# A new order for the projection phase of a linear-attention and SwiGLU block, and other queues for its first weights

## The chip, the cores and the metric

The kernel runs on one core of a Trainium2 chip. The metric is the device time of one execution in microseconds (us); of a kernel's runs the median is taken. Less is better.

## The reference

Two branches read the same 2048 rows of 512 bf16 values, and their sum with the rows themselves is the output.

```python
def _A_ref(x, wqkv, wo):                      # x is layernormed
    H = 32; Dh = D // H
    q, k, v = ...                             # (x @ wqkv), 32 heads of 16
    phi = lambda t: jnp.where(t > 0, t + 1, jnp.exp(t)) + 1e-6
    pq, pk = phi(q), phi(k)
    kv = jnp.einsum("bhsd,bhse->bhde", pk, v)
    z = jnp.einsum("bhsd->bhd", pk)
    num = jnp.einsum("bhqd,bhde->bhqe", pq, kv)
    den = jnp.einsum("bhqd,bhd->bhq", pq, z)[..., None] + 1e-6
    return (num / den).transpose(...).reshape(B, S, D) @ wo

def _B_ref(x, w_gate, w_up, w_down):          # F = 1792
    return (jax.nn.silu(x @ w_gate) * (x @ w_up)) @ w_down

xn = _layernorm(x)
return x + _A_ref(xn, ...) + _B_ref(xn, ...)
```

## The kernel before

The 2048 rows are 16 tiles of 128 (t = 0 to 15). The program is a list of operations, each for one engine, with the keys that it reads and writes; `_Program` turns the keys into semaphore waits, and every engine runs its operations in the order of the list. So the order in the list is the order on each of the five engines and in its DMA queue. An operation stands still until what it reads is there, and all that is behind it on its engine stands still with it.

There are two phases. Phase 1 normalises the tiles, projects them to Q and K, applies phi and accumulates G = xn^T phi(K) over all tiles in four banks of PSUM (banks 0 to 3). Phase 2 walks through 56 pairs (gate and up, eight matmuls each; four chunks of 512 rows by 14 chunks of F), turns G into the attention's matrix on the way, and adds both branches per output tile.

Phase 1 is one text of words, run from left to right by `run`. A word is a letter and a tile number, with chunks of the contraction behind a colon where not all four are meant. The letters that matter here:

- SyncE's DMA queue: `l` loads a tile of x. `D` transposes a normalised tile by DMA (L396) into xnT. `T` loads a large weight: T0 and T4 the halves of w_gate, T1 and T5 those of w_up (896 KB each), T2 the V part of wqkv, T3 wo (512 KB each), T6 w_down (1792 KB).
- VectorE: `S` is a tile's statistics (bn_stats L251 and bn_aggr L254). `L` normalises a tile (L315). `C` subtracts the mean. `u` and `s` make phi(Q) and phi(K) (L457) out of the projection's bank and the clamped exp. `g`, `f` and `w` copy transposed rows out of PSUM, `a` writes the negated mean as a row (L365 with VectorE).
- ScalarE: `R` makes the inverse deviation (L258, L260), `r` further powers of it (L265, L267, L269), `y` and `x` are the exps of Q and K (L436 for tiles 0 to 2, L439 for the others), `e`, `h` and `Y` copy transposed rows out of PSUM (L388, L353), `M` a negated mean (L272).
- GpSimd: `n` and `m` clamp the exps of Q and K (L446), `P` normalises a tile (L330 and L333), `J` makes the scaled rows that G needs for tiles 0 to 2, `O` is `a` on GpSimd.
- TensorE: `c` turns a tile of x by a matmul with the identity (L371), `d` adds the negated mean to that (L379), `W` and `X` transpose (L345), `K` and `Q` are the projections (L418, one matmul for each of four chunks of the contraction), `G` is the accumulation (L467, four matmuls), `F` is a filler of 256 columns (L241), `U` is one of phase 2's pairs done ahead (L521).

Tiles 0 to 2 ("centred") are projected before they are scaled by the inverse deviation: the exp takes the deviation as its scale and bias. Tiles 0 and 2 are transposed on TensorE as raw x, tiles 1 and 3 there after centring or normalising, and tiles 4 to 15 by DMA. For phase 2 the tiles 0 to 2 are normalised later too and turned by D0, D1 and D2. U0 needs the columns of tiles 0 to 3.

A projection takes the next of the banks 4 to 7 in turn (K and Q of tile 2 use banks 0 and 1), so it waits until the `s` or `u` of the projection four places back has read that bank. G of a tile waits for its `s`. The first G waits for banks 0 to 3, which the tiles at the start have used.

The first loads are six each on SyncE's and ScalarE's queues: tiles 0 to 3 of x and the four chunks (128 rows of wqkv by 512 columns, 128 KB) of the Q and of the K weights. A word Q1 in that list is chunk 1 of Q's weights. Ahead of all of it on TensorE, seven fillers of 512 columns (L241) run while the first loads are under way.

Of the kernel before, what the change touches and what calls it, by code (L numbers as in the profile page):

```python
# [111 lines left out]
def bass_parallel_sum__linear_attn_block__swiglu_ffn__prompt_kernel(nc, A_x, A_wqkv, A_wo, B_x, B_w_gate, B_w_up, B_w_down, out):  # L112
# [5 lines left out]
    with contextlib.ExitStack() as es:  # L118
        E = es.enter_context

        def sb(name, shape, dtype):
            return E(nc.sbuf_tensor(name, shape, dtype))
# [3 lines left out]
        r2 = sb("r2", [P, NC], f32)  # L126
# [59 lines left out]
        def xload(eng, t):  # L186
            load(eng, ("x", t), x_sb[:, t, :], xin[t * P:(t + 1) * P, :])
# [22 lines left out]
        def wchunk(eng, i, c):  # L210
            load(eng, ("wqk", i, c), wqkv[:, c, i * D:(i + 1) * D], A_wqkv[c * P:(c + 1) * P, i * D:(i + 1) * D])

        for eng, text in (("sp", "x0 x2 Q1 x3 Q2 K1"),
                          ("act", "x1 Q0 Q3 K0 K3 K2")):
            for w in text.split():
                if w[0] == "x":
                    xload(eng, int(w[1:]))
                else:
                    wchunk(eng, int(w[0] == "K"), int(w[1:]))
# [331 lines left out]
        def run(text):  # L551
            words = [(w[0], int(w[1:].split(":")[0]), [int(c) for c in w.split(":")[1]] if ":" in w else None)
                     for w in text.split()]
            late = {t for k, t, _ in words if k == "z"}
            later.update({t: i for i, t in enumerate(t for k, t, _ in words if k == "u" and t in late)})
            for k, t, cs in words:
                steps[k](t) if cs is None else steps[k](t, cs)

        run("""
            S0 c0 l13 M1 R0 O0 l5 d0 S2 F1 l4 F1 l11 O2 S1 r0 e0 h0 R2 c2 d2 Q0:01 g2 Q0:3 Q2:1 h2 Q2:3 C1 J0 W1  # L560
            S3 r2 J2 R1 l14 K0:0 Q0:2 Q2:2 Q2:0 K2:3 r1 w1 K0:3 K2:1 K0:1 R3 L3 J1 T1 y0 K0:2 n0 y2 K2:02 l9 S13
            n2 l10 X3 x0 x2 S4 u0 K1:23 K1:01 R13 m0 s0 Y3 m2 P13 u2 x1 Q1:012 s2 Q1:3 R4 y1 Q3 m1 S9 K3:13
            K3:02 l7 l12 R9 y3 G2 s1 D13 L1 G0 P4 D4 L9 n1 n3 G1 K13 u1 x3 m3 Q13 u3 s3 S5 x13 D9 m13 S7 y13 R5
            s13 K4 l8 x4 G3 S10 P5 K9 m4 s4 x9 D5 n13 m9 Q4 G13 y4 G4 u13 R10 S14 K5 R14 n4 L10 R7 Q5 s9 L7 l15
            l6 x5 P14 Q9 D1 u4 y5 G9 S6 D10 D14 m5 K10 s5 R6 n5 P6 D7 L2 S11 Q10 u5 D6 y9 G5 D2 x10 y10 n9 m10
            T2 K14 u9 P0 s10 x14 K7 n10 S12 R11 u10 m14 x7 m7 T3 Q6 S8 y6 R12 G10 K6 s14 R8 P12 D12 n6 x6 Q7 s7
            S15 L8 R15 G7 m6 u6 y7 s6 Q14 y14 D8 G14 Q12 P11 K12 n7 u7 y12 Q8 L15 x12 n14 n12 D0 m12 u14 D11 K8
            u12 s12 y8 n8 G6 G12 x8 K11 u8 m8 D15 s8 Q11 x11 K15 T0 Q15 y11 G8 x15 m11 T5 s11 y15 n11 m15 G11 T4
            u11 T6 n15 s15 u15 U0 G15 U1
        """)  # L570

        def gt_evac(c, eng):
# [181 lines left out]
```

## Time and profile before

| | us |
|---|---|
| median of 3 runs | 212.77 (212.51 to 212.78) |
| profiled execution, its own time | 212.57 |
| span of its instructions | 211.3 |
| TensorE busy | 207.0 |
| VectorE busy | 124.5 |
| ScalarE busy | 68.4 |
| GpSimd busy | 67.2 |

PE is TensorE's matmul side, PEld its weight loads, DVE is VectorE, ACT ScalarE, POOL GpSimd and SP SyncE; SPq and ACTq are the DMA issues of these queues. Lines are numbered as in the kernel above. In a timeline a row has the start and the length in us, the engine, line and operation, what it writes and reads, the shape, the count, and in brackets the idle time before it with what ended it. A matmul's length contains its way through the array, so the next one starts earlier than the row before it ends; spacing is read from start to start. In a row of waits stand who waited for whom, the total in us, how often, and the longest. In a row of DMA issues the last number is the median time from issue to landing.

Phase 1 ends on TensorE with U0 (from 47.77 us), G15 and U1 (from 50.35 us).

### The profile page before, as it was taken

The numbers are of one execution on the slowest core, as the hardware profiler recorded it, in microseconds if no ns is written. First come the engines' busy times: TensorE is split into PE (matmuls) and PEld (weight loads), VectorE is DVE, ScalarE is ACT, GpSimd is POOL, SyncE is SP. The second block draws the span as 40 slices with busy tenths as digits, with TensorE's granted clock in tenths as the row PEclk, the third lists the DMA queues.
The fourth block names the chain that finished last, engine by engine and source line by source line (L and its number), as shares of the span: only waits on it lengthen the run. The fifth ranks groups of instructions, "written<-read, shape, count | busy, mean of one in ns | idle before, by whom it ended". The sixth has DMA issues, their size and how long they took to land.

```text
span 211.3 us, 2728 instructions
## 1 busy us (share of the span) xinstructions
PE 207.0 (98%) x994; PEld 97.0 (46%) x1013; DVE 124.5 (59%) x223; ACT 68.4 (32%) x146; POOL 67.2 (32%) x95
## 2 busy tenths in 40 slices
PE   7999999999999999999999999999999999999996
PEld 3534444444544444444444444444444444444455
DVE  3799998653996368454644673464457463625122
ACT  5994656554344333031221322130123031220000
POOL 3795688649950162202102021202202210000000
DMA  5963557599501201110101110111001111011101
GB/s 157 364 200 78 124 102 225 101 343 365 161 0 25 53 0 25 25 50 28 25 25 36 38 29 25 25 46 28 28 25 26 25 50 50 3 50 26 49 28 50
DMA packets 28733, 16.43 MB, mean 78 GB/s; under 512 B 18608, under 2 KB 28592, under 8 KB 28720
## 3 DMA queue, kind: packets, MB, share of 16 engines
q1 hardware_dynamic: 27856, 15.48, 26.2%
q10 hardware_dynamic: 864, 0.79, 1.1%
q8 instruction: 8, 0.13, 0.3%
q14 instruction: 5, 0.04, 0.1%
HBM read 9.96 MB, written 2.10 MB: 57 GB/s over the span
## 4 chain that ended last, share of the span: by engine, by line
PE 94%; ACT 3%; DMA 1%; issue 1%; DVE 1%; POOL 0%
PE pb L521 46%; PE pb L655 23%; PE pb L418 11%; PE pb L651 7%; PE pb L467 7%; ACT ef L436 1%; DMA x_sb<-in_A_x_dram 1%; PE pb L579 0%; PE pb L379 0%; PE pb L645 0%; DVE stats L251 0%; ACT rstd L260 0%; ACT lnv L258 0%; ACT xnT L353 0%; PE pb L241 0%
## 5 line engine op out<-in xcount | busy, mean ns | idle before, releaser
L529 ACT ACTIVATE sil<-pb 128x512 bf16<-128x512 f32 x56 | 33.4, 597 | 104.1 <-PE pb L521 102.5
L534 DVE TENSOR_TENSOR hT<-pb,sil 128x512 bf16<-128x512 f32 x56 | 38.2, 683 | 38.1 <-PE pb L521 37.5
L521 PE MATMUL pb<-xnT,wg 128*128 128x512 bf16 x224 | 57.8, 379 | 0.0
L521 PE MATMUL pb<-xnT,wu 128*128 128x512 bf16 x214 | 55.8, 379 | 0.5
L655 PE MATMUL pb<-wd,hT 128*128 128x512 bf16 (+2 forms) x247 | 51.1, 355 | 0.3
L612 POOL TENSOR_TENSOR pz<-pq,zbc 128x512 f32<-128x512 bf16 x16 | 22.2, 1392 | 91.4 <-DVE den L619 79.4
L655 PEld LDWEIGHTS pb<-wd,hT 128*128 128x128 bf16 x252 | 23.5, 98 | 25.0
L521 PEld LDWEIGHTS pb<-xnT,wu 128*128 128x128 bf16 x224 | 21.9, 98 | 25.9
L521 PEld LDWEIGHTS pb<-xnT,wg 128*128 128x128 bf16 x224 | 21.9, 98 | 25.8
L661 DVE TENSOR_TENSOR out_sb<-pb,x_sb 128x512 bf16<-128x512 f32 (+2 forms) x18 | 11.4, 632 | 35.7 <-PE pb L655 35.7
L418 PE MATMUL pb<-wqkv,xnT 128*128 128x512 bf16 x102 | 23.8, 379 | 0.5 <-ACT xnT L353 0.4
L439 ACT ACTIVATE ef<-pb 128x512 bf16<-128x512 f32 x26 | 15.3, 593 | 12.5 <-PE pb L418 12.5
L446 POOL TENSOR_SCALAR ef<-ef 128x512 bf16<-128x512 bf16 x26 | 16.0, 617 | 8.6 <-ACT ef L439 8.6
L651 PE MATMUL pb<-M,pk 128*128 128x512 bf16 (+2 forms) x72 | 16.8, 355 | 0.0
L418 PEld LDWEIGHTS pb<-wqkv,xnT 128*128 128x128 bf16 x104 | 10.1, 98 | 12.9 <-ACT xnT L353 0.9
L467 PE MATMUL pb<-pk,xn 128*128 128x512 bf16 x51 | 12.8, 379 | 0.1
L251 DVE BATCH_NORM_STATS2 stats<-x_sb 128x6 f32<-128x512 bf16 x16 | 10.8, 678 | 3.4 <-DMA x_sb<-in_A_x_dram 3.4
L634 DVE TENSOR_TENSOR pq<-pq,rden 128x512 bf16<-128x512 bf16 x16 | 12.6, 785 | 0.0
L619 DVE TENSOR_REDUCE den<-pz 128x32 f32<-128x512 f32 x16 | 10.8, 676 | 0.0
L490 POOL TENSOR_TENSOR zacc<-zacc,pk 128x512 f32<-128x512 f32 x8 | 10.2, 1278 | 0.6
L457 DVE SCALAR_TENSOR_TENSOR pk<-pb,ef 128x512 bf16<-128x512 f32 x13 | 8.8, 679 | 2.6 <-POOL ef L446 2.6
L457 DVE SCALAR_TENSOR_TENSOR pq<-pb,ef 128x512 bf16<-128x512 f32 x13 | 8.8, 683 | 2.5 <-POOL ef L446 2.4
(70 smaller groups left out, 112.6 us busy)
## 6 DMA issues: line engine op xcount, KB each, us to landing
x_sb<-in_A_x_dram SPq DMA_DIRECT2D x15, 128.0 KB, 4.7
out_dram<-out_sb SPq DMA_DIRECT2D x15, 128.0 KB, 1.7
wu<-in_B_w_up_dram SPq DMA_DIRECT2D x2, 896.0 KB, 6.8
wg<-in_B_w_gate_dram SPq DMA_DIRECT2D x2, 896.0 KB, 7.0
wd<-in_B_w_down_dram SPq DMA_DIRECT2D x1, 1792.0 KB, 14.6
wqkv<-in_A_wqkv_dram ACTq DMA_DIRECT2D x5, 128.0 KB, 4.7
wqkv<-in_A_wqkv_dram SPq DMA_DIRECT2D x1, 512.0 KB, 3.9
wo<-in_A_wo_dram SPq DMA_DIRECT2D x1, 512.0 KB, 4.8
```

The lines of the kernel that those rows point to most:

```text
L418: fns.append(lambda e, c=c, first=first, last=last: e.matmul(banks[b][:, :], src[:, c, t * P:(t + 1) * P], wqkv[:, c, col:col + D], start= ...
L439: K.add("act", lambda e: e.activation(buf, banks[b][:, :], ACT.Exp), r=[B(b)], w=[bkey])
L446: K.add("pool", lambda e: e.tensor_scalar(out=buf, in0=buf, scalar1=top, scalar2=0.0, op0=ALU.min, op1=ALU.max), r=[bkey] + tkeys, w=[bkey])
L457: K.add("dve", lambda e: e.scalar_tensor_tensor(out=dst, in0=val, scalar=low, in1=mid, op0=ALU.max, op1=ALU.add), r=keys + lkeys, w=[dkey])
L467: K.add("pe", [(lambda e, c=c: e.matmul(banks[c][:, :], src[:, t, c * P:(c + 1) * P], pk[:, t, :], start=first, stop=last)) for c in range ...
L521: fns.append(lambda e, c=c, b=b, w_=w_: e.matmul(banks[b][:, :], w_[:, c, fc * P:(fc + 1) * P], xnT[:, c, C * 512:(C + 1) * 512], start=(c ...
L529: K.add("act", lambda e: e.activation(sil[:, j % 2, :], banks[gb(j)][:, :], ACT.Silu), r=[B(gb(j))], w=[("sil", j % 2)])
L534: K.add("dve", lambda e: e.tensor_tensor(out=hT[:, C % 2, fc, :], in0=banks[gb(j) + 1][:, :], in1=sil[:, j % 2, :], op=ALU.mult), r=[B(gb( ...
L612: K.add("pool", lambda e: e.tensor_tensor(out=pz[:, t % 2, :].rearrange("q (g p) -> q g p", g=NG), in0=pq[:, t, :].rearrange("q (g p) -> q ...
L634: K.add("dve", lambda e: e.tensor_tensor(out=heads(pq[:, t, :]), in0=heads(pq[:, t, :]), in1=rden[:, i, :][:, :, None].broadcast_to([P, NH ...
L651: fns = [(lambda e, g=g: e.matmul(banks[bank][:, 0:hi - lo], pk[:, t, g * P:(g + 1) * P], M[:, g, lo:hi], start=(g == 0), stop=False)) for ...
L655: fns = [(lambda e, fc=fc: e.matmul(banks[bank][:, 0:hi - lo], hT[:, C % 2, fc, jj * P:(jj + 1) * P], wd[:, fc, lo:hi], start=False, stop= ...
```

## The change

Two lists of words are replaced by others; no function is changed. In the list of the first loads, Q2 goes from SyncE to ScalarE, K2 from ScalarE to SyncE, and K1, K0 and K3 change their places. The text of phase 1 has another order, and these words differ:

- one of two fillers `F1` is gone, the other stands ahead of `c0`;
- the negated mean of tile 2 is made by VectorE (`a2`) and not by GpSimd (`O2`);
- of the four copies of turned rows of tiles 0 and 2, the first half of tile 0 goes from ScalarE to VectorE (`e0` to `g0`), and of tile 2 the first half from VectorE to ScalarE (`g2` to `e2`) and the second from ScalarE to VectorE (`h2` to `f2`);
- tiles 1 and 10 are normalised by GpSimd (`P1`, `P10` for `L1`, `L10`), tile 0 by VectorE (`L0` for `P0`).

Q0 and Q2 with K0 and K2 are cut into chunks in another order; Q1, K1, Q3 and K3 are mostly whole. The order of the large weights was T1, T2, T3, T0, T5, T4, T6, with the transposes D12, D8, D0, D11 and D15 between T3 and T0. It becomes T1, T0, T3, T4, T2, T6, T5, all but T1 behind D11, with D0 between T4 and T2. U0 stood ahead of G15 and U1 behind it; now all G stand ahead of U0.

```diff
-        for eng, text in (("sp", "x0 x2 Q1 x3 Q2 K1"),
-                          ("act", "x1 Q0 Q3 K0 K3 K2")):
+        for eng, text in (("sp", "x0 x2 Q1 x3 K1 K2"),
+                          ("act", "x1 Q0 Q3 Q2 K0 K3")):
...
         run("""
-            S0 c0 l13 M1 R0 O0 l5 d0 S2 F1 l4 F1 l11 O2 S1 r0 e0 h0 R2 c2 d2 Q0:01 g2 Q0:3 Q2:1 h2 Q2:3 C1 J0 W1
-            S3 r2 J2 R1 l14 K0:0 Q0:2 Q2:2 Q2:0 K2:3 r1 w1 K0:3 K2:1 K0:1 R3 L3 J1 T1 y0 K0:2 n0 y2 K2:02 l9 S13
-            n2 l10 X3 x0 x2 S4 u0 K1:23 K1:01 R13 m0 s0 Y3 m2 P13 u2 x1 Q1:012 s2 Q1:3 R4 y1 Q3 m1 S9 K3:13
-            K3:02 l7 l12 R9 y3 G2 s1 D13 L1 G0 P4 D4 L9 n1 n3 G1 K13 u1 x3 m3 Q13 u3 s3 S5 x13 D9 m13 S7 y13 R5
-            s13 K4 l8 x4 G3 S10 P5 K9 m4 s4 x9 D5 n13 m9 Q4 G13 y4 G4 u13 R10 S14 K5 R14 n4 L10 R7 Q5 s9 L7 l15
-            l6 x5 P14 Q9 D1 u4 y5 G9 S6 D10 D14 m5 K10 s5 R6 n5 P6 D7 L2 S11 Q10 u5 D6 y9 G5 D2 x10 y10 n9 m10
-            T2 K14 u9 P0 s10 x14 K7 n10 S12 R11 u10 m14 x7 m7 T3 Q6 S8 y6 R12 G10 K6 s14 R8 P12 D12 n6 x6 Q7 s7
-            S15 L8 R15 G7 m6 u6 y7 s6 Q14 y14 D8 G14 Q12 P11 K12 n7 u7 y12 Q8 L15 x12 n14 n12 D0 m12 u14 D11 K8
-            u12 s12 y8 n8 G6 G12 x8 K11 u8 m8 D15 s8 Q11 x11 K15 T0 Q15 y11 G8 x15 m11 T5 s11 y15 n11 m15 G11 T4
-            u11 T6 n15 s15 u15 U0 G15 U1
+            F1 M1 c0 l13 S0 O0 S2 a2 R0 d0 r0 g0 c2 d2 R2 h0 e2 Q0:0 Q0:1 Q0:3 Q2:01 S1 Q0:2 r2 C1 R1 S3 r1 J0
+            W1 l4 K0:1 K2:01 l11 R3 J2 l9 f2 w1 Q2:3 Q2:2 l10 l14 K0:2 K0:0 K0:3 y0 L3 y2 l5 J1 K2:2 K2:3 X3 T1
+            n0 K1 n2 x0 S13 S4 x2 u0 m0 s0 l12 Y3 R13 m2 l8 u2 Q1 P13 K3 D13 x1 s2 Q3:2 S9 y1 R4 m1 Q3:013 s1 R9
+            G0 G2 x3 P4 S5 L9 y3 n1 G1 m3 u1 n3 D4 D9 K13 l6 P1 x13 R5 s3 u3 Q13 S14 R14 K4 G3 x4 y13 m13 Q4 s13
+            y4 S10 K9 S6 P5 m4 n13 l7 R10 R6 x9 n4 P10 G13 s4 G4 u13 S7 u4 D5 m9 s9 K5 D10 R7 S12 L7 P14 D14 Q5
+            x5 m5 y5 Q9 y9 s5 n5 G9 K10 G5 u5 n9 K14 S11 S8 x10 R12 P6 D7 m10 l15 u9 Q10 P12 Q7 s10 R8 x14 L8 D6
+            y7 L2 R11 m14 K7 y10 x7 D1 G10 s14 S15 n7 R15 n10 u7 K6 m7 u10 G14 Q14 x6 D8 L15 K8 s7 m6 y14 s6 P11
+            x8 n14 Q8 D12 G7 y8 K12 D2 m8 x12 D15 L0 u14 Q12 D11 s8 n8 y12 u8 Q11 y11 T0 n12 K15 u12 T3 G6 x15
+            m12 s12 T4 D0 n11 G8 Q6 y6 K11 T2 x11 m15 u11 Q15 n6 s15 m11 G15 y15 n15 G12 u6 s11 u15 G11 U0 T6
+            U1 T5
         """)
```

## The prediction

> **What bounds the kernel now.** I read the page first: how busy each engine is, and the chain of work that ended last.
>
> ```profile
> span 211.3 us, 2728 instructions
> PE 207.0 (98%) x994; PEld 97.0 (46%) x1013; DVE 124.5 (59%) x223; ACT 68.4 (32%) x146; POOL 67.2 (32%) x95
> ...
> PE 94%; ACT 3%; DMA 1%; issue 1%; DVE 1%; POOL 0%
> ```
>
> TensorE is busy for 207.0 of 211.3 us and is 94% of the chain. The change adds no matmul, so it can gain only where PE stands still, waits at a slow clock, or does filler. The waits of PE name all the places:
>
> ```profile
> PE pb L241 <- PEq L739: 0.8, 1, 0.8
> PE pb L418 <- ACT xnT L353: 0.4, 1, 0.4
> PE pb L379 <- POOL nmb L365: 0.2, 1, 0.2
> ```
>
> The first is the start of the program. The other two lie in the first 13 us, which the timeline of PE shows (start, length, line, count):
>
> ```profile
> 3.78 0.63 PE L371 MATMUL pb<-ident,x_sb 128*128 128x128 bf16 x4
> 4.64 0.61 PE L379 MATMUL pb<-ident,nmb 128*128 128x256 bf16 x2 [0.23 <-POOL nmb L365]
> 5.04 0.63 PE L241 MATMUL pb<-const-bfloat16-1.0 128*128 128x256 bf16 x2
> ...
> 5.89 0.46 PE L379 MATMUL pb<-ident,nmb 128*128 128x256 bf16 x2
> 6.19 1.24 PE L418 MATMUL pb<-wqkv,hT 128*128 128x512 bf16 x5
> ...
> 10.09 1.89 PE L418 MATMUL pb<-wqkv,hT 128*128 128x512 bf16 x7
> 12.36 1.90 PE L418 MATMUL pb<-wqkv,xnT 128*128 128x512 bf16 x8 [0.37 <-ACT xnT L353]
> 14.10 2.75 PE L467 MATMUL pb<-pk,hT 128*128 128x512 bf16 x12
> ...
> 47.77 1.03 PE L521 MATMUL pb<-xnT,wg 128*128 128x512 bf16 x4
> ...
> 50.35 1.03 PE L521 MATMUL pb<-xnT,wg 128*128 128x512 bf16 x4
> ```
>
> From 47.77 to 50.35 twelve matmuls start (U0's eight, G15's four), 0.215 us each, so a group of four (one K, Q or G word) costs 0.863 us with the few hundredths between instructions. From 12.36 on the groups follow without a hole. The row at 10.09 holds eight matmuls (K1 and Q1, one record missing), so PE had issued everything by 10.09 + 8 x 0.216 = 11.82 and lost 0.54 us until 12.36; the view says 0.37 because it counts from a matmul's modelled end. That wait was for tile 3's transposed rows (Y3 on ScalarE). The second loss is the filler: two F1 at 5.04, the next useful matmul at 5.47, so 0.43 us.
>
> **The filler.** One F1 goes; the other moves ahead of c0. There it costs about half of 0.43, 0.21 us, and c0 starts at 3.99 instead of 3.78. d0 waits for the mean row from GpSimd until 4.64 in any case, and that idle 0.23 us hides the moved F1 (without that cover it would cost 0.21). d0 stays at 4.64, c2 starts at 5.04 instead of 5.47: **gain 0.43**, if d2's mean row is there. It is now made by VectorE (a2) behind the second aggregate:
>
> ```profile
> 4.91 0.18 DVE L254 BATCH_NORM_AGGREGATE mv<-stats 128x2 f32<-128x6 f32 x1
> 6.29 0.42 DVE L390 CAST hT<-pb 128x256 bf16<-128x256 f32 x1 [0.40 <-PE pb L379]
> ```
>
> The trace has no such operation on VectorE. Its nearest row is this aggregate, also one column, 0.18 us; from below it could be half of that, from above twice. So a2 ends at 5.2 to 5.5, I take 5.3, and d2 wants it at 5.47. g0, the 0.42 us cast, follows it and ends near 5.7, before Q0:0 wants it at 5.87.
>
> **The slow clock.** d0's two matmuls take 0.40 us (4.64 to 5.04); d2's two, of the same shape, 0.30 (5.89 to 6.19), and the first projections behind them 0.216 each. PE's clock doubles at about 6.1 us. What moves ahead of that moment is done at the slow rate: d2 costs 0.40 and starts at 5.47, Q0:0 starts at 5.87 and takes 0.32 instead of 0.22. **Loss 0.21.** The remaining order needs the same matmuls and transposes, so PE has issued Q1's last at 11.60 instead of 11.82.
>
> **The weight chunks.** The order now uses the chunks as it dealt them:
>
> ```profile
> 1.25 2.39 ACTq L184 DMA_DIRECT2D wqkv<-in_A_wqkv_dram  x5
> 2.67 0.91 SPq L184 DMA_DIRECT2D wqkv<-in_A_wqkv_dram  x2
> ...
> wqkv<-in_A_wqkv_dram SPq DMA_DIRECT2D x3, 128.0 KB, 4.7
> ```
>
> Every chunk has 128 KB, so I let a slot keep its landing: issue plus 4.7 us. Q2 goes from SyncE's fifth slot (2.67, lands 7.4) to ScalarE's fourth (2.2, lands 6.9) and is wanted at 7.05; K1 takes the fifth slot, lands at 7.4 and is wanted at 7.5; K0 lands at about 7.6, wanted 7.7. Margins are 0.1 to 0.2 us; a chunk 0.3 late costs at most 0.2. I take nothing.
>
> **The wait at 12.36.** It ends with ScalarE's evacuation of tile 3:
>
> ```profile
> 5.32 0.63 ACT L388 ACTIVATE hT<-pb 128x256 bf16<-128x256 f32 x2
> 5.85 0.29 ACT L258 ACTIVATE lnv<-mv,eps 128x1 f32<-128x1 f32 x1
> 6.39 0.38 ACT L388 ACTIVATE hT<-pb 128x256 bf16<-128x256 f32 x1
> ...
> 8.63 2.77 ACT L436 ACTIVATE ef<-pb,lstd,rstd 128x512 bf16<-128x512 f32 x4
> 11.28 0.30 ACT L258 ACTIVATE lnv<-mv,eps 128x1 f32<-128x1 f32 x1
> ...
> 11.72 0.58 ACT L353 ACTIVATE xnT<-pb 128x512 bf16<-128x512 bf16 x1
> ```
>
> Before: e0 and h0 (0.53 for two), R2 (0.54), h2. After: R2 at 5.32, at the 0.44 that R13 takes (11.28 to 11.72), then h0 and e2 at 0.27 each: r2 can start at 6.30, where before h2's 0.27 ended at 6.66. ScalarE is 0.36 ahead and its next steps are the same, so the four exps start at 8.27 and end at 10.92 (0.66 each), and Y3 now stands before R13: 10.92 + 0.58 = 11.50, plus the 0.06 from 12.30 to PE's start at 12.36. PE's first use, K3, comes at 11.60. **The whole 0.54 goes**, with 0.04 to spare.
>
> K3 and Q3 then end at 13.33. G0 needs the banks that u2 and s2 free. Exps, minima and sums of tiles 0 and 2 keep their order, so s2 should end 0.36 sooner than before. VectorE before:
>
> ```profile
> 8.76 0.41 DVE L315 TENSOR_SCALAR xn<-x_sb,mv,rstd 128x512 bf16<-128x512 bf16 x1 [0.63 <-ACT rstd L260]
> ...
> 12.87 0.74 DVE L457 SCALAR_TENSOR_TENSOR pk<-pb,flo,ef 128x512 bf16<-128x512 f32 x1
> 13.53 0.68 DVE L251 BATCH_NORM_STATS2 stats<-x_sb 128x6 f32<-128x512 bf16 x1
> ...
> 14.35 0.72 DVE L457 SCALAR_TENSOR_TENSOR pk<-pb,flo,ef 128x512 bf16<-128x512 f32 x1
> 14.98 1.35 DVE L315 TENSOR_SCALAR xn<-x_sb,mv,rstd 128x512 bf16<-128x512 bf16 x2
> ```
>
> That makes 12.87 + 0.74 - 0.36 = 13.25. Next late after Y3, then, is s2, less than 0.1 us ahead of PE.
>
> **Sum of the head:** 0.43 - 0.21 + 0.54 = 0.76 us; the first G starts at 13.33 instead of 14.10.
>
> **The middle, to 48 us.** Both orders hold the same groups, so any loss must be a new wait. The tightest I find is Q13, whose bank Q1 leaves only when u1 has been summed. VectorE after: s2 at 12.51, S9 13.17, s1 13.99, S5 14.65, L9 15.47 (0.66 a sum, 0.82 a pair of statistics, from start to start as in those rows). L9 costs 0.41 as at 8.76 or half of 1.35 as at 14.98; u1's 0.74 ends at 16.6 or 16.88, and PE arrives at 13.33 + 4 x 0.863 = 16.78: no wait, or 0.1. The Trainium skill, page "SBUF — State Buffer", section "Who interferes with whom", says that VectorE in its two-port modes and GpSimd exclude each other for a whole instruction: by that rule the slow row holds, since GpSimd has m3 to do there, and 0.1 would be lost. I take 0.07, near the slow row, which stands at the same place of the old order. One normalisation less on VectorE (L1 and L10 go to GpSimd as P1 and P10, P0 comes back as L0) helps the same stretch; on GpSimd P1 stands ahead of m13, but s13 is wanted only by K9, four groups or 3.4 us after K13's end. P10 stands ahead of m9, whose sum s9 is wanted by G9, four groups behind K9. The last sum, s11, has Q15, G15 and G12 between K11 and G11, 2.6 us, against the 0.66 of an exp and the 0.74 of a sum with a minimum between them. I found no other place with less than 0.2 us (K4 behind s3).
>
> **Forecast.** 0.76 - 0.07 = 0.7 us. The profiled execution took 212.57 (span 211.3 and 1.27 around it), so 211.87; the median of the runs, 212.77, stands 0.20 over it, so **212.05**. 0.2% is 0.43 us, about what a measurement of this kernel can tell from no change.
>
> **Rival 1: the vector chain takes it back.**
>
> ```profile
> 15.00:35.00 20.00, 19.89 (x92) 9.04 (x93) 19.27 (x40) 12.52 (x34) 14.44 (x27) 1.00 0.52 128
> ```
>
> In this row of 20 us (busy PE, weight loads, DVE, ACT, POOL) VectorE works for 19.27. If it can't come 0.7 sooner, small waits return 0.4 to 0.7 of the gain; with 0.5 the time is 212.55. Against it speaks that its load falls and its first part is 0.36 ahead; for it, that margins are tenths. 16%.
>
> **Rival 2, slower: D0 stuck behind weights.** Before, T0 is the last but three on SyncE and D0 had gone long before it. Now the order is D11, T0, T3, T4, D0, and U0 needs tile 0's columns.
>
> ```profile
> 34.41 6.45 SPq L396 DMA_TRANSPOSE xnT<-xn  x5
> 40.91 0.58 SPq L184 DMA_DIRECT2D wg<-in_B_w_gate_dram  x1
> ...
> 42.08 0.51 SPq L184 DMA_DIRECT2D wg<-in_B_w_gate_dram  x1
> ...
> wg<-in_B_w_gate_dram SPq DMA_DIRECT2D x1, 896.0 KB, 5.2
> ...
> wg<-in_B_w_gate_dram SPq DMA_DIRECT2D x1, 896.0 KB, 8.8
> ...
> wd<-in_B_w_down_dram SPq DMA_DIRECT2D x1, 1792.0 KB, 14.6
> ...
> 35.84 0.77 POOL L333 TENSOR_SCALAR xn<-x_sb,nm,rstd 128x512 bf16<-128x512 bf16 x1
> ```
>
> P11 stands behind m6, and K6 is the 23rd group behind 13.33 and ends at 33.2; with an exp, a minimum and the 0.77 of the last row, xn of tile 11 is there near 35.8, 0.8 sooner than before; a transpose takes SyncE 1.29 (6.45 for five), so T0 is issued at 37.1, lands 5.2 later at 42.3, T3 1.4 later (two loads of 896 KB landed 46.1 and 50.9 with one between: 2.4 each, so 1.4 for 512 KB), T4 at 46.1, D0 by 47.4. U0 comes at 13.33 + 40 x 0.863 = 47.9: hidden by 0.5. The Trainium skill, page "DMA: Bandwidth & Descriptors", section "Queues, rings and completion order", says that one queue's descriptors are consumed in ring order on each DMA engine, by which D0 can't overtake T4. If T0 goes out 1 us later and each load takes a third longer, as wd's 1792 KB did (57.2 - 50.9 = 6.3 by the last DMA row), D0 lands near 50, PE loses 2 us, and the time is 212.05 + 2 = 214.0, slower. It decides from a landing at 47.9, and turns the sign from 48.6. The load that is now last, T5, is no such case: the last before, wd, landed at about 42.6 + 14.6 = 57.2; T0 goes 3.8 sooner, T2 and T3 with 2.8 us of bytes come behind it, so T5 lands near 56 to 57, and its first user, the eighth pair of the second phase, comes 7 x 1.73 behind U0, at 60. 13%.
>
> **Rival 3: it doesn't do what it says.** Y3 or a chunk comes 0.3 late and half of the 0.54 stays: 212.05 + 0.27 = 212.3, still faster. 12%.
>
> **How the numbers follow.** Forecast 59%, the rivals 16, 13 and 12. Low end: 0.76 off the lowest run shown, 212.51, so 211.75. High end: rival 1 at its worst and the first 0.1 of a loss, 212.85. Faster 0.70: the forecast and rival 3. Same 0.15: rival 1. Slower 0.15: rival 2 and the worst of rival 1.
>
> **What would show it.** L241 once at 3.8, c2 near 5.04; Y3's evacuation near 10.9 and ahead of L258; no wait of PE for xnT before L467, which starts near 13.3; second-phase gate matmuls (L521) of U1 near 49.6. Wrong: a PE wait for DVE between 14 and 45, or one for the transposes (L396) ahead of L521 near 48.

## The result and the profile after

The changed kernel takes 211.96 us (median of 6 runs, 211.80 to 212.02) against 212.70 before (6 runs, 212.51 to 212.78). The ratio is 0.9966, with a 95% interval from 0.9953 to 0.9978: faster by 0.34%, against the 0.34% that 212.05 meant. A second series gave 211.94 against 212.56, a ratio of 0.9967 (0.9956 to 0.9978). So the medians differ by 0.74 us in the first series and by 0.62 in the second. The profiled execution took 212.02, 0.55 less than that of before.

The page of the changed kernel, three lines:

```profile
span 210.7 us, 2744 instructions
...
PE 207.8 (99%) x1012; PEld 96.6 (46%) x1012; DVE 124.4 (59%) x224; ACT 68.0 (32%) x145; POOL 67.8 (32%) x96
...
PE 97%; DMA 1%; DVE 1%; issue 0%
```

ScalarE and GpSimd have left the chain. The waits of PE, all that the view names:

```profile
PE pb L241 <- PEq L739: 0.8, 1, 0.8
PE pb L379 <- DVE nmb L365: 0.2, 1, 0.2
```

The wait for xnT is gone, and a short one for VectorE's mean row (a2) is new. The timeline of PE:

```profile
3.99 0.63 PE L371 MATMUL pb<-ident,x_sb 128*128 128x128 bf16 x4
...
4.83 0.39 PE L371 MATMUL pb<-ident,x_sb 128*128 128x128 bf16 x4
5.42 0.39 PE L379 MATMUL pb<-ident,nmb 128*128 128x256 bf16 x2 [0.20 <-DVE nmb L365]
5.75 1.73 PE L418 MATMUL pb<-wqkv,hT 128*128 128x512 bf16 x6
...
7.62 2.33 PE L418 MATMUL pb<-wqkv,hT 128*128 128x512 bf16 x10
...
11.73 1.89 PE L418 MATMUL pb<-wqkv,xnT 128*128 128x512 bf16 x8
13.46 0.81 PE L467 MATMUL pb<-pk,hT 128*128 128x512 bf16 x3
...
47.99 1.03 PE L521 MATMUL pb<-xnT,wg 128*128 128x512 bf16 x4
...
49.72 1.03 PE L521 MATMUL pb<-xnT,wg 128*128 128x512 bf16 x4
```

K3 starts at 11.73, where before the first matmul on tile 3 came at 12.36: 0.63 us. The first G is 0.63 ahead (13.46 for 14.10) and U1 is 0.63 ahead (49.72 for 50.35). PE's last matmuls, too, are 0.64 ahead (a row at 207.91 for one at 208.55). So in these two executions all of the gain is made by 11.73 us, and neither the middle nor the end changes it. ScalarE, then VectorE, in their timelines:

```profile
5.71 0.64 ACT L388 ACTIVATE hT<-pb 128x256 bf16<-128x256 f32 x2
...
8.24 2.79 ACT L436 ACTIVATE ef<-pb,lstd,rstd 128x512 bf16<-128x512 f32 x4
10.91 0.60 ACT L353 ACTIVATE xnT<-pb 128x512 bf16<-128x512 bf16 x1
11.39 0.31 ACT L258 ACTIVATE lnv<-mv,eps 128x1 f32<-128x1 f32 x1
```

```profile
5.21 0.16 DVE L365 TENSOR_SCALAR nmb<-mv 128x1 bf16<-128x1 f32 x1
...
12.50 0.74 DVE L457 SCALAR_TENSOR_TENSOR pk<-pb,flo,ef 128x512 bf16<-128x512 f32 x1
...
15.42 0.59 DVE L315 TENSOR_SCALAR xn<-x_sb,mv,rstd 128x512 bf16<-128x512 bf16 x1
15.94 0.74 DVE L457 SCALAR_TENSOR_TENSOR pq<-pb,flo,ef 128x512 bf16<-128x512 f32 x1
```

Y3 (L353) ends at 11.51, 0.22 ahead of K3. Its chain no longer decides; what does is told below.

### The profile page after: what moved, and what is told of

It reads as the page before. It is cut to its first block, busy times and chain, and to the rows that moved or that the text cites. A ratio compares the mean times of both kernels' runs of the same rounds, so it can differ in the third digit from the quotient of the medians.

```text
span 210.7 us, 2744 instructions
## 1 busy us (share of the span) xinstructions
PE 207.8 (99%) x1012; PEld 96.6 (46%) x1012; DVE 124.4 (59%) x224; ACT 68.0 (32%) x145; POOL 67.8 (32%) x96
## 4 chain that ended last, share of the span: by engine, by line
PE 97%; DMA 1%; DVE 1%; issue 0%
PE pb L521 46%; PE pb L655 23%; PE pb L418 13%; PE pb L651 7%; PE pb L467 7%; DMA x_sb<-in_A_x_dram 1%; DVE stats L251 1%; PE pb L579 0%; PE pb L645 0%; PE pb L345 0%; PE pb L379 0%; DVE mv L254 0%; DVE out_sb L661 0%; DVE nmb L365 0%
## 5 line engine op out<-in xcount | busy, mean ns | idle before, releaser
L521 PE MATMUL pb<-xnT,wu 128*128 128x512 bf16 x224 | 57.8, 379 | 0.0
L651 PEld LDWEIGHTS pb<-M,pk 128*128 128x128 bf16 x72 | 6.8, 98 | 7.4
```

The costliest lines, as they stand in the source:

```text
L521: fns.append(lambda e, c=c, b=b, w_=w_: e.matmul(banks[b][:, :], w_[:, c, fc * P:(fc + 1) * P], xnT[:, c, C * 512:(C + 1) * 512], start=(c ...
L651: fns = [(lambda e, g=g: e.matmul(banks[bank][:, 0:hi - lo], pk[:, t, g * P:(g + 1) * P], M[:, g, lo:hi], start=(g == 0), stop=False)) for ...
```

## The experiments

Each experiment has its own runs of the kernel before on the same chip; their medians lay between 212.56 and 212.62.

**One word of the old order.** Y3 ahead of R13, nothing else:

```diff
-K1:23 K1:01 R13 m0 s0 Y3 m2 P13
+K1:23 K1:01 Y3 R13 m0 s0 m2 P13
```

> The kernel before with one word moved: Y3 ahead of R13. Theory (the gain is the wait for tile 3's rows, ended by ScalarE): Y3 starts at 11.28 instead of 11.72, PE's first use comes at 11.92 instead of 12.36, so 0.44 us sooner; 212.7 becomes 212.26. Rival (the gain comes from the order of the middle, with one normalisation less on VectorE, and the wait at 12.36 is made up for later): within 0.1 of 212.7.

Measured 212.25, ratio 0.9982 (0.9973 to 0.9991). The timelines of ScalarE and of PE:

```profile
11.28 0.60 ACT L353 ACTIVATE xnT<-pb 128x512 bf16<-128x512 bf16 x1
```

```profile
11.94 1.90 PE L418 MATMUL pb<-wqkv,xnT 128*128 128x512 bf16 x8
13.68 1.67 PE L467 MATMUL pb<-pk,hT 128*128 128x512 bf16 x7
...
50.14 1.03 PE L521 MATMUL pb<-xnT,wg 128*128 128x512 bf16 x4
```

Y3 and PE's first use come when they were expected (11.28 and 11.92). Half of the change's gain, 0.37 of 0.74 us, is to be had by this one move, and the wait for tile 3 is shown to have cost time. In this execution not all of it is kept: the first G is 0.42 ahead of the kernel before, U1 only 0.21 (50.14 for 50.35), because two projections of the old middle now wait for their transposes (0.05 us at 26.68, 0.14 at 37.19).

**The fillers alone.**

```diff
-S0 c0 l13 M1 R0 O0 l5 d0 S2 F1 l4 F1 l11
+F1 S0 c0 l13 M1 R0 O0 l5 d0 S2 l4 l11
```

> The kernel before with the change's fillers alone: one F1 gone, the other ahead of c0. Theory: PE comes to the wait for tile 3's rows 0.2 to 0.4 us sooner and waits there that much longer, because ScalarE's chain is as before: 212.7, no change within 0.1. Rival (fillers are a term of their own, as the sum in the prediction has them, 0.43 less 0.21): 212.5 or less.

Measured 212.46, ratio 0.9993 (0.9984 to 1.0002): not to be told from no change. The number alone does not decide: 212.46 lies where the rival had it, but it is only 0.16 below the 212.62 of the kernel before beside it. The profiled execution is the slowest of the eleven (212.69), and its timeline of PE shows where the freed time went:

```profile
5.57 0.64 PE L379 MATMUL pb<-ident,nmb 128*128 128x256 bf16 x2
6.49 1.18 PE L418 MATMUL pb<-wqkv,hT 128*128 128x512 bf16 x4 [0.29 <-ACT rstd L260]
```

d2's two matmuls would be issued by 6.0, and the first projections start at 6.49: the missing fillers have become a wait there, earlier than the one expected at tile 3. The trace puts it down to rstd, which those projections do not read; they want chunk Q1, which landed at 6.36 in this execution (at 6.00 in the profile of before).

**Both together.**

> Both edits of the two kernels beside it. Theory: Y3 ends at 11.86 and PE comes to it earlier than that, so the first K3 or Q3 starts at 11.92 as with Y3 alone, and G2 stays behind s2 (end 13.61) at 13.66: 212.26, no better than Y3 alone by over 0.1. Rival (the terms add): 212.26 less 0.2 to 0.4, so about 212.0.

Measured 212.52, ratio 1.0001 (0.9983 to 1.0019; one run at 214.54 makes the interval wide). The terms do not add, but 212.26 is missed too. In its profile the first projections start at 6.58, behind a chunk that landed at 6.45. Whether the fillers' absence makes the old head worse or these executions had late landings stays open.

**The filler back in the new order.**

```diff
-S2 a2 R0 d0 r0 g0 c2 d2
+S2 a2 R0 d0 F1 r0 g0 c2 d2
```

> The changed kernel with the second F1 put back between d0 and c2. Theory (PE waits for a2 and for the chunks in any case): 0.1 to 0.2 us of filler fall into those waits, 211.96 within 0.1. Rival (the filler's time is a term of its own): 0.2 more, 212.2 or above.

Measured 212.11, ratio 0.9975 (0.9966 to 0.9984): 0.15 over the changed kernel's 211.96, between the two expectations and not to be told from either. PE in its profile:

```profile
5.05 0.42 PE L241 MATMUL pb<-const-bfloat16-1.0 128*128 128x256 bf16 x1
5.26 0.63 PE L371 MATMUL pb<-ident,x_sb 128*128 128x128 bf16 x4
5.69 0.63 PE L379 MATMUL pb<-ident,nmb 128*128 128x256 bf16 x2
6.11 1.57 PE L418 MATMUL pb<-wqkv,hT 128*128 128x512 bf16 x6
...
13.62 0.59 PE L467 MATMUL pb<-pk,hT 128*128 128x512 bf16 x2
```

Here c2's four matmuls still run slowly (0.63, where the changed kernel's take 0.39), the first projection starts 0.36 later (6.11 for 5.75), and the first G only 0.16 later (13.62 for 13.46), as much as K1's chunk landed later (7.73 for 7.57).

**The halves of the change.** The new order up to the first G, and the old one behind it:

```diff
 ... Q3:2 S9 y1 R4 m1 Q3:013 s1 R9
-G0 G2 x3 P4 S5 L9 y3 n1 G1 m3 u1 n3 D4 D9 K13 ...
+y3 G2 l7 L1 G0 P4 D4 L9 n1 n3 G1 K13 u1 x3 m3 ...
```

> The new order up to the first G with the new queues, and the old order from there on (L1, L10, P0 and the old places of the large weights and of U0). Theory (all of the gain is in the first 13.5 us): 212.0 to 212.15; up to 0.15 may go where K4 now takes the bank that s3 frees last. Rival (the middle and the end bring it): 212.5 or more.

Measured 212.94, ratio 1.0014 (1.0005 to 1.0022). It is not faster: the theory's number is too low by 0.8 to 0.9 us. The waits of PE:

```profile
PE pb L418 <- DMA wqkv<-in_A_wqkv_dram: 0.5, 1, 0.5
PE pb L418 <- DMA xnT<-xn: 0.4, 1, 0.4
```

In this execution a late chunk spoiled the head (K1 landed at 8.11, first G at 14.01), but the rest lost time as well: from the first G to U1 it took 36.96 us (14.01 to 50.97) where before took 36.26 (14.10 to 50.35). 0.17 of that is K4's wait for s3, and the rest K10's wait for its transpose D10 (the second row; from start to start it is 0.51). D10 landed 3.24 us after its issue, where in the kernel before it took 2.49. There two other transposes took as long (D14 3.34, D7 3.25), and PE did not wait for them; why one lands later than another was not followed.

The seam also makes something that is in neither order: l7, which the old order has ahead of D13 and the new one behind D9, stands between D13 and D4, and D4 lands at 18.34 (17.48 before, 17.35 in the changed kernel). So what this half loses is not shown to be the old order's doing alone. The other half, the old head with the new rest:

> The old order and queues up to the first G, and the new order from there on. Theory (the gain is in the head alone): 212.7 within 0.1. Rival (the middle brings part of it): 212.5 or less.

Measured 212.55, against 212.60 of the kernel before beside it, ratio 1.0002 (0.9994 to 1.0011): nothing, as the theory had it. From the first G (14.04) to U1 (50.30) it takes 36.26 us, exactly as before: both orders of the middle are dense when PE comes as late as before. So neither half is faster by itself. The new head wins the time; the old rest, as it is joined on here, hands it back, and the new rest keeps it.

**Which words keep it.** D1 behind D10 and D14, and in a second kernel also P1 for L1:

```diff
-x5 P14 Q9 D1 u4 y5 G9 S6 D10 D14 m5
+x5 P14 Q9 u4 y5 G9 S6 D10 D14 D1 m5
```

```diff
-G2 l7 L1 G0 P4 D4 L9 n1 n3 G1
+G2 l7 G0 P4 D4 L9 n1 n3 P1 G1
```

> The kernel with the new head and the old rest, with one word moved: D1 behind D10 and D14 instead of ahead of them in SyncE's queue. Theory (that kernel lost its gain at K10, which waited for D10 behind D1, a transpose that only phase 2 needs): D10 is issued 1.25 us sooner, the wait of 0.5 us or more goes, 212.94 becomes 212.2 to 212.45. Rival (the late chunk at 8.16 us of its profile was the loss): 212.9.

> The same with P1 behind n3 on GpSimd instead of L1 on VectorE. Theory (the other wait, 0.17 us of K4 for s3, comes from L1's 0.74 us on VectorE ahead of u1, u3 and s3): it goes too, 212.05 to 212.25. Rival (P1 puts GpSimd's minima late instead): no better than D1 alone.

Measured 212.84 (ratio 1.0013, 1.0002 to 1.0024) and 212.93 (1.0019, 1.0010 to 1.0027). Both theories fall. The first rival's 212.9 is met, but not for its reason: no chunk was late in this profile, the first G starts at 13.57. With D1 moved the wait at K10 is gone, but the chain finds the next places. PE loses 0.28 us at 18.16, where D4, the transpose behind l7, landed at 18.02 and s3 ended at 18.00, and 0.34 at three later ones, all of them transposes. So U1 starts at 50.43, 0.08 later than before, though the first G came 0.53 sooner. In the second kernel, with P1 ahead of m3, it is the rival's way: the first G is at 13.24, 0.86 sooner than before, and U1 at 50.53, 0.18 later. Its waits of PE, then VectorE's timeline:

```profile
PE pb L418 <- DVE pk L457: 0.5, 1, 0.5
```

```profile
17.47 0.69 DVE L457 SCALAR_TENSOR_TENSOR pk<-pb,ef 128x512 bf16<-128x512 f32 x1 [0.85 <-POOL ef L446]
```

VectorE idles 0.85 us ahead of s3 for a minimum that GpSimd does behind P1, and K4 waits 0.5 for that s3. The new order has P1 behind m3. Which set of its moves is needed to keep the gain is not settled; these two are not enough, and all three of these kernels have l7 at the seam.

**The queues.** The changed kernel with the old lists of first loads:

```diff
-("sp", "x0 x2 Q1 x3 K1 K2"), ("act", "x1 Q0 Q3 Q2 K0 K3")
+("sp", "x0 x2 Q1 x3 Q2 K1"), ("act", "x1 Q0 Q3 K0 K3 K2")
```

> The changed kernel with the chunks of Q and K on the old queues. Theory (PE takes each chunk within 0.1 us of its landing): Q2 lands at about 7.57 and K1 at 8.0 instead of 7.04 and 7.57, so K0:1 starts at about 8.07 instead of 7.62 and nothing behind it has that much to spare: 0.45 us more than the changed kernel, 212.4. Rival (the clock and the order of the engines set the head, the deal is cover only): 212.0.

Measured 212.44, ratio 0.9999 (0.9990 to 1.0008): the 212.4 that was expected. But its profile does not show the expected wait. The chunks landed up to 0.9 us early in it (K1 at 7.27), and PE's clock turned late:

```profile
5.12 0.63 PE L371 MATMUL pb<-ident,x_sb 128*128 128x128 bf16 x4
5.55 0.63 PE L379 MATMUL pb<-ident,nmb 128*128 128x256 bf16 x2
5.98 1.89 PE L418 MATMUL pb<-wqkv,hT 128*128 128x512 bf16 x6
7.71 0.39 PE L345 MATMUL pb<-ident,hT 128*128 128x128 bf16 x4
...
13.77 0.59 PE L467 MATMUL pb<-pk,hT 128*128 128x512 bf16 x2
```

From 4.72 on PE has no hole here, c2 and d2 run at the slow rate, and so do the first two of the six projections from 5.98 (0.43 us each, 0.22 behind them). The first G starts at 13.77, 0.31 later than in the changed kernel, with no wait to put it down to: in this execution the slow clock held the head. So the kernel ran again, beside the changed one.

> The changed kernel with the old queues once more, because the chunks of its first profile landed up to 0.9 us sooner than in all the others. Theory: with landings as usual (fifth slot 7.4 to 8.1) its K0:1 waits for K1 until about 8.1 and the first G starts at 13.9, 0.4 later than the changed kernel beside it; the median is 0.3 to 0.5 above it. Rival (the deal does nothing): the same as the changed kernel within 0.1.

> The changed kernel once more, beside the three others on one chip. Both theories: 211.96 within 0.15. Theory (the head is held by landings and not by the clock): the first G starts at 13.3 to 13.7 whenever PE's clock turns. Rival (the slow clock is a term, as the prediction had it): a turn 1.5 us later than the 4.6 us of the first profile costs 0.2 to 0.7 and the first G follows it one for one.

Measured 212.53, ratio 1.0000 (0.9989 to 1.0010), and 211.94 for the changed kernel: 0.59 apart. Without the new queues little or nothing of the new order's gain is left. That is shown by the medians; the wait of K0:1 for K1 itself is in neither profile, since in the second one tile 2 of x came late and PE waited there. For the theory speak the landings of all profiles; K1 is here chunk 1 of K's weights, and K0:1 the projection of tile 0 that first wants it. With the old queues K1 landed at 7.97 to 8.59 us in six of seven, with the new ones at 7.03 to 8.11. And in five of the seven with the new queues K0:1 starts 0.05 us behind K1's landing, and the first G 5.84 to 5.87 behind K0:1:

| kernel | K1 lands | K0:1 starts | first G |
|---|---|---|---|
| D0 further behind (below) | 7.48 | 7.53 | 13.38 |
| changed, first profile | 7.57 | 7.62 | 13.46 |
| new head, D1 moved | 7.65 | 7.70 | 13.57 |
| filler back | 7.73 | 7.78 | 13.62 |
| new head, old rest | 8.11 | 8.16 | 14.01 |

In the third and the fourth of these c2 and d2 ran at the slow rate throughout, and the first G follows K1's landing all the same. In the two that are left PE was not waiting for K1: with P1 moved it landed early (7.03), and in the profile of the changed kernel that ran beside, the slowest of its seven runs, x2 came late. The PE of that one:

```profile
3.99 0.55 PE L371 MATMUL pb<-ident,x_sb 128*128 128x128 bf16 x4
4.48 0.39 PE L379 MATMUL pb<-ident,nmb 128*128 128x256 bf16 x2
5.30 0.40 PE L371 MATMUL pb<-ident,x_sb 128*128 128x128 bf16 x4 [0.43 <-DMA x_sb<-in_A_x_dram]
6.44 0.39 PE L379 MATMUL pb<-ident,nmb 128*128 128x256 bf16 x2 [0.74 <-DVE nmb L365]
...
14.20 1.03 PE L467 MATMUL pb<-pk,hT 128*128 128x512 bf16 x4
```

The same kernel, and again an early clock; x2 lands at 5.25 instead of 4.24, d2 starts 1.02 later than in the first profile (6.44 for 5.42), the first G 0.74 later (14.20 for 13.46), the execution takes 212.76 instead of 212.02, 0.74 longer. The expected 13.3 to 13.7 is missed. A late landing moves the head and the execution by the same 0.74. The rival, a late clock, is not tried by this profile, because the clock turned early in it. The table speaks against it, and the first profile with the old queues for it: landings hold the head in most of these executions, and the clock where the landings are early enough.

**D0 further behind.**

```diff
-T4 D0 n11 G8 Q6 y6 K11 T2 x11
+T4 n11 G8 Q6 y6 K11 T2 T5 D0 x11
...
-U1 T5
+U1
```

> The changed kernel with D0 behind T2 and T5 too (order T0, T3, T4, T2, T5, D0, T6). Theory (a transpose lands behind the loads ahead of it in its queue, as the second rival of the prediction had it): T2 lands at 47.7, T5 at 50.1, D0 at about 50.6 instead of 46.8, U0 at 50.7 instead of 48.0, so 2.7 us more: 214.7. Rival (a transpose passes the loads): 212.0.

Measured 214.65 in the profiled execution and 214.45 in one other, both at a granted clock of 1.0. The four others took 216.27 to 217.75 at a granted clock of 0.992, which makes the median 216.32; what lowered the clock was not followed. The waits of PE and its timeline:

```profile
PE pb L521 <- DMA xnT<-xn: 2.5, 1, 2.5
```

```profile
50.62 1.04 PE L521 MATMUL pb<-xnT,wg 128*128 128x512 bf16 x4 [2.54 <-DMA xnT<-xn]
```

U0 starts at 50.62, against 50.7 expected; D0 landed at 50.57, 0.5 us behind T5 (50.08). Here a transpose lands behind the loads ahead of it; the second rival's mechanism is real.

## Why the prediction was right

*Where the gain lies, and the wait for tile 3.* Right. ScalarE's order was worth what the steps said: exps at 8.24 (8.27 predicted), Y3 at 10.91 (10.92), s2 at 12.50 (12.51). Y3 alone gave 0.37 us on the old order, of the 0.44 expected of it.

*The filler.* Half right. F1 ahead of c0 was hidden, and a2 took 0.16 and ended at 5.37 (5.3 predicted). But 0.43 was no term that stands by itself: freed alone it became a wait in the execution that was profiled, and put back in the new order the filler costs about 0.15, which can't be told from nothing.

*The slow clock, a loss of 0.21.* This term was not there in the profiled execution. The clock turned before 4.83 (0.39 for c2's four transposes), PE came to d2 too early, and the time went into waits: 0.2 us for a2, then for the chunks. Nor is it always absent: in the first profile with the old queues the clock turned at about 6.8 us, and nothing else held the head.

*The chunks, taken at nothing.* Mis-sized: K1 landed at 7.57, not 7.4, K0:1 started at 7.62 instead of 7.5, and from there PE had no hole. This is the 0.13 by which K3 came later than predicted (11.73 for 11.60), and the sum of the head is 0.63 instead of 0.76. So a loss that did not come and waits that were not priced partly cancel in the sum, and that the forecast of 0.7 met the 0.74 of the medians so closely (0.62 in the second series) is in part luck.

*The middle, a loss of 0.07.* It was 0: u1 started at 15.94, 0.52 behind L9, between the quick and the slow row, ended at 16.68, and Q13 came at 13.46 + 4 x 0.863 = 16.91. The Trainium skill's rule for VectorE beside GpSimd (page "SBUF — State Buffer", section "Who interferes with whom") is so borne out in its direction: beside GpSimd's minima, L9 took 0.59 us and not 0.41. A stop for a whole instruction of GpSimd, 0.61 us, is not what this row shows. One count was off, to the safe side: between K9 and G9 stand five groups and not four. That any loss must be a new wait proved the important sentence: with the old rest joined to the new head these waits eat the whole gain.

*The second rival.* It didn't come about, by a wider margin than foreseen. SyncE's timeline and its DMA issues:

```profile
37.20 0.58 SPq L184 DMA_DIRECT2D wg<-in_B_w_gate_dram  x1
...
38.38 0.51 SPq L184 DMA_DIRECT2D wg<-in_B_w_gate_dram  x1
38.93 1.63 SPq L396 DMA_TRANSPOSE xnT<-xn  x1
...
42.58 4.86 SPq L184 DMA_DIRECT2D wu<-in_B_w_up_dram  x1
```

```profile
wg<-in_B_w_gate_dram SPq DMA_DIRECT2D x1, 896.0 KB, 5.1
...
wg<-in_B_w_gate_dram SPq DMA_DIRECT2D x1, 896.0 KB, 7.9
...
xnT<-xn SPq DMA_TRANSPOSE x1, 7.9
```

T0 at 37.2 (37.1 predicted), landed 42.3 (42.3), T4 at 46.3 (46.1), D0 at 38.93 + 7.9 = 46.8 (by 47.4), U0 at 47.99 (47.9): hidden by 1.2 us, where 0.5 was foreseen. D0 lands 0.5 us behind T4, which agrees with the ring order of the Trainium skill's page "DMA: Bandwidth & Descriptors", section "Queues, rings and completion order". That D0 can't overtake T4 is the prediction's own step from it; in neither profile did it. With D0 further behind it landed 3.75 us later (50.57 for 46.82); 1.2 of that was hidden, and U0 and the execution came 2.63 later, one for one from there, as that rival's working had it.

## What to carry to other kernels

Where one engine is 97% of the chain, cost a reordering from that engine's few waits: for each, what ends it, and what would end it next. Then follow the time that is won down the rest of the order: a rest that was just dense can hand it back in new waits, because what it waits for does not come sooner by as much. In the profile of Y3 alone the first G was 0.42 us sooner, but D10 landed only 0.04 sooner and D12 0.23 later, and 0.21 was kept to U1; the new head with the old rest was slower than before. And treat times freed at one place as bounds and not as a sum: a filler taken out ahead of a load that has not landed buys a wait.

## What the runs showed of the hardware that was not expected

First loads land at different times from run to run, with the same issue: x2 took 3.0 us in the first profile of the changed kernel and 4.0 in the second, the chunk in SyncE's fifth slot 4.9 and 5.3, and 4.0 in a profile with the old queues. In five profiles the head follows one chunk's landing to 0.05 us, so this is a part of each kernel's spread.

PE's clock turns at no fixed time. In the second profile with the old queues c0's four transposes are fast at 3.96 us; in the first, with the same kernel, the two projections from 5.98 still take 0.43 us each, and only at about 6.8 do they take 0.22 (its rows stand in the part on the queues):

```profile
3.96 0.39 PE L371 MATMUL pb<-ident,x_sb 128*128 128x128 bf16 x4
```

The first G starts at 13.87 and 13.77 in the two: in the second profile x2 came late, and the early clock was of no use. The Trainium skill, page "TensorE: Matmul & The Clock Gate", section "Part 1: The HAM clock gate (the "warmup" mystery)", calls the window that decides free-running and gives about half a microsecond either way; the traces agree that it is not tied to the kernel's start, but show a spread of almost 3 us, from 3.9 to 6.8.

A DMA issue can block its queue for long: T5's took SyncE 4.86 us in the changed kernel, as the row at 42.58 shows, with T0, T3, T4, D0, T2 and T6 ahead of it. Nothing behind it was urgent.
